# Masked scores computed in quadrants, with k transposed and the states in quarters, in a gated linear attention and SiLU block kernel

## The chip, the cores and the metric

One Trainium2 chip, one of its NeuronCores. The metric is device time in microseconds of the one launch that computes everything, median of several runs. Inside the core, TensorE (PE) multiplies matrices into PSUM, VectorE (DVE) and ScalarE (ACT) do elementwise work and empty PSUM, GpSimd (POOL) sets constants, and SyncE (SP) issues the transfers. Each engine works through its own queue in order; they meet at semaphores.

## The reference

A gated linear attention over 4 batch rows, 8 heads, 768 positions and 48 channels, and then a two-layer block with SiLU over the 3072 tokens. All of it is float32 in the kernel; the weights arrive as float64.

```python
state = np.zeros((B, H, D, D))
for t in range(S):
    state = alpha[:, :, t, :, None] * state + np.einsum('bhd,bhe->bhde', k[:, :, t], v[:, :, t])
    y[:, :, t] = np.einsum('bhd,bhde->bhe', q[:, :, t], state)
x = y.transpose(0, 2, 1, 3).reshape(B * S, H * D)      # 3072 x 384
h = x @ w_in                                           # 384 x 2048
g = h * (1.0 / (1.0 + np.exp(-h)))
out = g @ w_out                                        # 2048 x 384
```

## The kernel before

**Attention, by chunks.** The sequence is cut into six pieces of C = 128 positions; with four batch rows there are NT = 24 chunks, numbered n = 4 ci + b, so that the four batch rows of one piece follow one another. The eight heads are handled as NP = 4 pairs: head 2j of pair j lies in partitions 0 to 47, head 2j + 1 in partitions 64 to 111 (u = 0 and 1). For a chunk, four stages follow one another:

- `products` and `quotient` (from L652): running products of alpha along the 128 positions (a scan on VectorE), and from them kp and qp, k and q scaled so that the product of qp at position t with kp at position s contains the right decay. Both lie channels by positions.
- `scores` (L706): for each pair j and head u a matmul kp by qp gives the 128 x 128 scores, s on the partitions and t on the columns, in two PSUM banks (one for each u, four pairs side by side). L719 copies them out to `g`, multiplied by `mask`, which is 1 where t >= s. For all but the last piece of a batch row, L723 then transposes kp (positions on the partitions) and ScalarE copies it to `kn` (L725). L729 scales the running state `st`.
- `values` (L734): y transposed, channels on the partitions, in groups of 32: v by g, and for ci > 0 `st` by qp on top (L749). ScalarE copies it to `xt` (L754), the input of the second part.
- `states` (L755): kn by v (L764) is added to `st` (L770, VectorE).

`load_v` (L475) brings v of a chunk, positions on the partitions, in one transfer into one of NV = 2 buffers.

**The block of two layers.** The second part is multiplied in groups of four chunks. The first two groups use plain products (`enter_plain`, L807); the later ones use a scheme with fewer products and more sums (`enter`, L830, with VectorE sums at L844, ScalarE copies at L836 and SiLU at L841). The output side is `leave` (L928; L955 for the first half group).

**PSUM.** Eight banks: three for attention (`ps_a`, given out in turn by `ps_attn`), three for the first layer (`ps_m`), two for the output (`ps_o`).

**Order.** A loop over 25 steps runs the stages in four slots; the list `stages` says which stage stands in which slot and for which chunk (lag 1 is the chunk before). After each slot, `fill` issues pieces of the two-layer block until it has kept pace with a due amount. In steps 0 to 3 the order is products, scores, values, states; in steps 4 to 7 scores, products, values, states, each in its own slot; from step 8 on values and states share a slot and the last one holds `quotient`. The queues of the engines follow this program order closely; the framework that builds the program may move an instruction ahead of one that it expects to wait.

Of the kernel before, what the change touches and what calls it, by code (L numbers as in the profile page):

```python
# [8 lines left out]
F32 = mybir.dt.float32  # L9
# [3 lines left out]
AF = mybir.ActivationFunctionType  # L13
ALU = mybir.AluOpType
# [341 lines left out]
def quotients(  # L356
# [22 lines left out]
    C = 128  # L379
# [4 lines left out]
    NKT = HD // 128  # L384
    NFT = DF // 128
    NT = B * NCH
    W = C + 1
    GB = 4
    NG = NT // GB
# [28 lines left out]
    def ps_attn(n=C):  # L418
        return ps_a.tile([128, 512], F32, name="ps_a").rearrange("p (j c) -> p j c", c=n)
# [54 lines left out]

    def load_v(n):  # L475
        c = ctxs.setdefault(n, dict(zip(("ci", "b"), divmod(n, B))))
        rows = slice(c["ci"] * C, c["ci"] * C + C)
        t = c["v"] = vns[n % NV]
        nc.sync.dma_start(t[:, :, 0:D], v[c["b"], :, rows, :].transpose([1, 0, 2]))

    early = []
    wide = moe_w_in.dtype != F32
# [26 lines left out]
    for t in [inv] + seg[1:]:  # L509
        gps.memset(t, 0.0)  # L510


    mask = consts.tile([128, C], F32, name="mask")
# [174 lines left out]
    def quotient(n, sg=None, q=None):  # L688
# [14 lines left out]
            turned(c["q"], q)  # L703
        dve.tensor_tensor(qp, q, qp, ALU.mult)

    def scores(n):  # L706
        c = ctxs[n]
        ci, b = c["ci"], c["b"]
        ps = [ps_attn() for _ in range(2)]


        for j in range(NP):
            for u in range(2):
                r = slice(64 * u, 64 * u + D)
                pe.matmul(ps[u][:, j, :], lhsT=c["kp"][r, j, :], rhs=c["qp"][r, j, :],  # L715
                          start=True, stop=True)
        g = c["g"] = work.tile([128, 2, NP, C], F32, name="g")
        for u in range(2):
            dve.tensor_tensor(g[:, u], ps[u], mask[:, None, :].to_broadcast([128, NP, C]), ALU.mult)  # L719
        if ci < NCH - 1:  # L720
            ps_k = ps_attn()
            for j in range(NP):
                pe.transpose(ps_k[:, j, :], c["kp"][:, j, :], ident)  # L723
            c["kn"] = work.tile([128, NP, C], F32, name="kn")
            act.copy(c["kn"], ps_k)  # L725
        if ci > 0:
            s = st[b].rearrange("p j u e -> p j (u e)")
            for j in range(NP):
                act.mul(s[:, j], s[:, j], c["all"][:, j : j + 1])  # L729
# [4 lines left out]
    def values(n):  # L734

        c = ctxs[n]
        ci, b, g, qp = c["ci"], c["b"], c["g"], c["qp"]
        vn = c["v"].rearrange("p (j u) d -> p j (u d)", u=2)
        s = st[b].rearrange("p j u e -> p j (u e)")
        py = ps_attn()  # L740
        todo = [(3 * j + i, vn[:, j, at : at + 32], g[:, u, j, :])
                for j in range(NP) for i, at, u in ((0, 0, 0), (1, 32, 0), (2, 80, 1))]
        todo += [(3 * j + 1, vn[:, j, 48:80], g[:, 1, j, :]) for j in range(NP)]
        if ci > 0:
            todo += [(3 * j + i, s[:, j, 32 * i : 32 * i + 32], qp[:, j, :])
                     for j in range(NP) for i in range(3)]
        for i, (at, w, x) in enumerate(todo):
            t, at = divmod(at, 4)
            pe.matmul(py[32 * at : 32 * at + 32, t, :], lhsT=w, rhs=x, start=(i < 4),  # L749
                      stop=(i >= len(todo) - 4), skip_group_check=True)  # L750
        half, e = divmod(n, 2)
        if e == 0:
            xts[half] = xtp.tile([128, NKT, TB], F32, name="xt")
        act.copy(xts[half][:, :, e * C : (e + 1) * C], py[:, 0:NKT])  # L754
    def states(n):  # L755
        c = ctxs.pop(n)
        ci, b, vn = c["ci"], c["b"], c["v"]
        if ci < NCH - 1:

            ps = ps_attn()  # L760
            for j in range(NP):
                for u in range(2):
                    r = slice(64 * u, 64 * u + D)
                    pe.matmul(ps[r, j, 0:D], lhsT=c["kn"][:, j, r], rhs=vn[:, 2 * j + u, 0:D],  # L764
                              start=True, stop=True)
# [378 lines left out]
    go_on()  # L1144
    go_on()
    ps = ps_attn()[0:1, 0, 0:1]
    pe.matmul(ps, lhsT=good, rhs=mask[:, C - 1 : C], start=True, stop=True)  # L1147
    dve.tensor_single_scalar(small, ps, 127.5, ALU.is_ge)
    for _ in range(4):
        go_on()  # L1150
# [60 lines left out]
```

## Time and profile before

| | |
|---|---|
| time, median of 3 | 577.69 us (577.37 to 578.81) |
| profiled span | 577.1 us, TensorE clock 1.000 |
| PE busy | 557.6 us, 4450 matmul records |
| VectorE busy | 449.3 us |
| ScalarE busy | 187.6 us |
| scores, L715: 384 records | 30.0 us, mean 292 ns |
| k transposed, L723: 80 records | 13.5 us, mean 293 ns |
| values, L749: 768 + 480 records | 28.8 + 17.0 us, means 282 and 272 ns |
| states, L764: 320 records | 11.9 us, mean 216 ns |
| masking, L719: 48 of 128 x 512 | 31.2 us, mean 685 ns |
| copy of kn, L725: 20 of 128 x 512 | 11.7 us, mean 585 ns |
| v, L479: 24 transfers of 192 KB | 3.5 us from issue to landing, median |

How to read it: PE is TensorE's matmuls, PEld its weight loads, which lie beside them. The means are those of one record from start to end; records overlap, so the time that a stretch takes is read from the starts in the timeline and not from the sum of the means. In the names of a group the output stands left of the arrow and the inputs right of it; `128*48 128x48` is the part of the array that is used (rows*columns) and the shape that streams through. In a table of waits, each line gives the engine and line that waited, whom it waited for, and then the total, the number of times and the longest.

### The profile page before, as it was taken

Reading aid. Unit: us, or ns where it says so; the run is one execution under the profiler, and the core shown is the slowest. Engines: PE = TensorE matmul, PEld = TensorE weight load, DVE = VectorE, ACT = ScalarE, POOL = GpSimd, SP = SyncE. Lnnn points to the kernel's source line nnn. Section 1 sums busy time; section 2 is a strip of 40 time slices with the busy share of each in tenths; the row PEclk is TensorE's granted clock in tenths of the full one; section 3 lists DMA queues with packets and bytes.
Section 4 is the critical chain, followed back from the end, with each engine's and each line's share of the span. In section 5 each row is a group of like instructions: output and inputs, shape, how many; then the busy total and the mean of one; then the engine's idle time right before and its main releaser. Section 6 shows DMA issues by size and latency. Waiting matters only on the chain. (4 is left out here: it accounts for less than half of the span.)

```text
span 577.1 us, 11060 instructions
## 1 busy us (share of the span) xinstructions
PE 557.6 (97%) x4450; PEld 491.2 (85%) x4450; DVE 449.3 (78%) x807; ACT 187.6 (33%) x367; POOL 7.3 (1%) x25
## 2 busy tenths in 40 slices
PE   5999999999999999999999999999999999998976
PEld 4677887678998998898998998998998999997976
DVE  5779798999797699995996995996963856747651
ACT  2345543232221233342442442433342331422100
POOL 5000000000000000000000000000000000000000
PEclk9999999999999999999999999999999999999999
DMA  9998784445445414343324333323210123333321
GB/s 212 169 285 215 212 215 118 102 103 139 103 99 129 116 51 120 107 124 84 103 71 118 101 105 85 101 69 89 65 43 9 52 81 115 93 118 98 98 72 30
DMA packets 93900, 63.72 MB, mean 110 GB/s; under 512 B 54800, under 2 KB 85520, under 8 KB 93840
## 3 DMA queue, kind: packets, MB, share of 16 engines
q1 hardware_dynamic: 93840, 62.94, 42.5%
q8 instruction: 36, 0.59, 0.4%
q14 instruction: 24, 0.20, 0.1%
HBM read 58.20 MB, written 4.72 MB: 109 GB/s over the span
## 5 line engine op out<-in xcount | busy, mean ns | idle before, releaser
L928 PE MATMUL ps_o<-w_out,g 128*128 128x192 f32 x704 | 122.8, 328 | 2.3 <-DVE o L942 2.2
L928 PEld LDWEIGHTS ps_o<-w_out,g 128*128 128x128 f32 x704 | 115.2, 190 | 5.6 <-DVE o L942 3.0
L928 PE MATMUL ps_o<-wt,g 128*128 128x192 f32 x528 | 91.6, 326 | 1.3 <-DVE u L1004 1.3
L807 PE MATMUL ps_m<-xt,w_in 128*128 128x256 f32 x384 | 89.6, 384 | 0.8 <-DVE w_in L604 0.5
L928 PEld LDWEIGHTS ps_o<-wt,g 128*128 128x128 f32 x528 | 87.2, 190 | 3.0 <-DVE u L1004 1.6
L807 PEld LDWEIGHTS ps_m<-xt,w_in 128*128 128x128 f32 x384 | 70.7, 190 | 12.2 <-DVE w_in L604 2.9
L830 PE MATMUL ps_m<-xc,w_in 128*128 128x256 f32 x288 | 70.1, 379 | 0.0
L639 DVE TENSOR_REDUCE seen<-bits 128x1 f32<-128x384 int32 (+2 forms) x65 | 42.4, 689 | 30.4 <-DMA bits<-in_moe_w_out_dram 23.9
L830 PEld LDWEIGHTS ps_m<-xc,w_in 128*128 128x128 f32 x288 | 54.0, 190 | 6.4 <-DVE g L844 0.2
L830 PE MATMUL ps_m<-xc,wx 128*128 128x256 f32 x192 | 50.1, 383 | 0.0
L836 ACT COPY g<-ps_m 128x512 f32<-128x512 f32 x64 | 37.0, 586 | 39.8 <-PE ps_m L830 39.8
L933 DVE TENSOR_TENSOR g<-g 128x512 f32<-128x512 f32 x66 | 44.7, 687 | 4.7 <-PE ps_o L928 4.7
L841 ACT ACTIVATE g<-g 128x1024 f32<-128x1024 f32 x32 | 33.2, 1056 | 44.6 <-DVE g L844 44.6
L729 ACT ACTIVATE st<-st,u 128x96 f32<-128x96 f32 x80 | 26.0, 368 | 53.5 <-DVE u L674 38.8
L844 DVE TENSOR_TENSOR g<-ps_m,g 128x512 f32<-128x512 f32 x56 | 37.6, 684 | 2.9 <-PE ps_m L830 2.7
L830 PEld LDWEIGHTS ps_m<-xc,wx 128*128 128x128 f32 x192 | 35.0, 190 | 4.2 <-issue 0.4
L719 DVE TENSOR_TENSOR g<-ps_a,mask 128x512 f32<-128x512 f32 x48 | 31.2, 685 | 6.4 <-PE ps_a L715 6.1
L674 DVE TENSOR_TENSOR_SCAN u<-al,one 128x516 f32<-128x516 f32 x24 | 29.3, 1224 | 6.2 <-ACT al L671 6.1
L699 DVE TENSOR_TENSOR_SCAN p<-al,inv 128x516 f32<-128x516 f32 x24 | 29.5, 1229 | 4.8 <-PE ps_a L749 4.2
L836 ACT COPY part<-ps_m 128x512 f32<-128x512 f32 x32 | 18.8, 587 | 43.6 <-PE ps_m L830 37.8
L810 ACT ACTIVATE g<-ps_m 128x512 f32<-128x512 f32 x32 | 19.0, 594 | 40.6 <-PE ps_m L807 40.5
L715 PEld LDWEIGHTS ps_a<-p,u 48*128 48x128 f32 x384 | 24.8, 193 | 8.1 <-issue 6.5
(117 smaller groups left out, 635.3 us busy)
## 6 DMA issues: line engine op xcount, KB each, us to landing
bits<-in_moe_w_in_dram SPq DMA_DIRECT2D x24, 512.0 KB, 4.2
bits<-in_moe_w_out_dram SPq DMA_DIRECT2D x32, 384.0 KB, 3.4
at<-in_alpha_dram SPq DMA_DIRECT2D x64, 96.0 KB, 2.3
kt<-in_k_dram SPq DMA_DIRECT2D x64, 96.0 KB, 2.4
qt<-in_q_dram SPq DMA_DIRECT2D x64, 96.0 KB, 2.5
vn<-in_v_dram SPq DMA_DIRECT2D x24, 192.0 KB, 3.5
bits<-in_alpha_dram SPq DMA_DIRECT2D x9, 512.0 KB, 3.9
out_dram<-o SPq DMA_DIRECT2D x48, 96.0 KB, 1.8
```

Source lines behind the costliest of these rows:

```text
L639: dve.tensor_reduce(seen[kind][which][:, i : i + 1], x, axis=AX, op=op, apply_absolute_value=True))
L674: dve.tensor_tensor_scan(u[:, end - 1 :: -1], sg[:, end:0:-1], one[:, end:0:-1], 0.0, ALU.mult, ALU.add)
L699: dve.tensor_tensor_scan(p[:, 0:end], sg[:, 0:end], iv[:, 0:end], 0.0, ALU.mult, ALU.add)
L719: dve.tensor_tensor(g[:, u], ps[u], mask[:, None, :].to_broadcast([128, NP, C]), ALU.mult)
L729: act.mul(s[:, j], s[:, j], c["all"][:, j : j + 1])
L807: pe.matmul(ps[:, e, :], lhsT=w_in[:, t, (f + e) * 128 : (f + e + 1) * 128], rhs=xt[:, t, :], start=(t == 0), stop=(t == NKT - 1))
L830: pe.matmul(ps[:, e], lhsT=block_w(w)[:, 2 * pair + e], rhs=block_x(grp, x), start=(first and e == 0), stop=(e == 1), skip_group_check=True)
L836: act.copy(to, ps)
L841: act.activation(x, x, AF.Silu)
L844: dve.tensor_tensor(to, a, b, op)
L928: pe.matmul(ps, lhsT=x, rhs=w[:, i], start=(first and i == 0), stop=(i == HF - 1), skip_group_check=True)
L933: dve.tensor_tensor(cells(grp, h, pair, *to), cells(grp, h, pair, *x), cells(grp, h, pair, *y), ALU.subtract)
```

## The change

Of the 128 x 128 scores of a head, the part with t < s is masked off; with s and t cut into halves, the block of late s and early t is masked off as a whole. The new form does not compute it. The two halves of s are two matmuls, e = 0 with all 128 columns of t and e = 1 with the last 64. Each uses 48 rows (one head) and 64 columns of the array, a quadrant. So that neither column half of the array gets all the long ones, the halves change places for odd pairs j: the s half e lies in partitions 64 (e ^ j % 2).

What follows from this:
- `mask` gets one version for even and one for odd pairs, and g has its rows swapped for odd pairs. So v must be swapped for odd pairs too, which `load_v` does with six transfers in place of one, and so must the rows of kn.
- The block that is not computed still has to be a finite number before the mask multiplies it by 0. A new stage `blank` takes the two score banks of a chunk ahead of time and has ScalarE write zeros to them. It stands behind `states` or `quotient` of the step before.
- kp is transposed in `values` now, ahead of the values' own matmuls and in the array's shape that these use (128 rows by 32 columns): matmuls with the identity, one for each quarter of the positions.
- The matmuls of `states` are cut to 32 columns as well, so that they have this shape too.

```diff
     def load_v(n):
         c = ctxs.setdefault(n, dict(zip(("ci", "b"), divmod(n, B))))
-        rows = slice(c["ci"] * C, c["ci"] * C + C)
+        x = v[c["b"], :, c["ci"] * C : c["ci"] * C + C, :].rearrange("(g o u) c d -> o g c u d", o=2, u=2)
         t = c["v"] = vns[n % NV]
-        nc.sync.dma_start(t[:, :, 0:D], v[c["b"], :, rows, :].transpose([1, 0, 2]))
+        to = t.rearrange("p (g o u) d -> o g p u d", o=2, u=2)[:, :, :, :, 0:D]
+        for g in range(NP // 2):
+            nc.sync.dma_start(to[0, g], x[0, g])
+            for e in range(2):
+                nc.sync.dma_start(to[1, g, CH * e : CH * e + CH], x[1, g, CH - CH * e : 2 * CH - CH * e])
...
+    mask = consts.tile([128, 2, C], F32, name="mask")
     gps.memset(mask, 1.0)
-    gps.affine_select(mask, mask, pattern=[[1, C]], compare_op=ALU.is_ge, fill=0.0, base=0,
-                      channel_multiplier=-1)
+    for odd in range(2):
+        for e in range(2):
+            m = mask[CH * e : CH * e + CH, odd, :]
+            gps.affine_select(m, m, pattern=[[1, C]], compare_op=ALU.is_ge, fill=0.0,
+                              base=-CH * (e ^ odd), channel_multiplier=-1)
...
+    def blank(n):
+        ps = ctxs[n]["blank"] = [ps_attn() for _ in range(2)]
+        for t in ps:
+            act.activation(t.rearrange("p j c -> p (j c)"), ident[:, 0:1].to_broadcast([128, 4 * C]),
+                           AF.Copy, scale=0.0)
+
     def scores(n):
...
-        ps = [ps_attn() for _ in range(2)]
+        ps = c.pop("blank")
         for j in range(NP):
-            for u in range(2):
-                r = slice(64 * u, 64 * u + D)
-                pe.matmul(ps[u][:, j, :], lhsT=c["kp"][r, j, :], rhs=c["qp"][r, j, :],
-                          start=True, stop=True)
+            for e in range(2):
+                for u in range(2):
+                    r = slice(64 * u, 64 * u + D)
+                    at, s = CH * (e ^ j % 2), CH * e
+                    pe.matmul(ps[u][at : at + CH, j, s:C], lhsT=c["kp"][r, j, s : s + CH],
+                              rhs=c["qp"][r, j, s:C], start=True, stop=True)
...
-        if ci < NCH - 1:
-            ps_k = ps_attn()
-            for j in range(NP):
-                pe.transpose(ps_k[:, j, :], c["kp"][:, j, :], ident)
-            c["kn"] = work.tile([128, NP, C], F32, name="kn")
-            act.copy(c["kn"], ps_k)
...
     def values(n):
...
+        if ci < NCH - 1:
+            ps_k = ps_attn()
+            for j in range(NP):
+                for i in range(4):
+                    at = 32 * (i ^ 2 * (j % 2))
+                    pe.matmul(ps_k[at : at + 32, j, :], lhsT=c["kp"][:, j, 32 * i : 32 * i + 32], rhs=ident,
+                              start=True, stop=True)
+            c["kn"] = work.tile([128, NP, C], F32, name="kn")
+            act.copy(c["kn"], ps_k)
         py = ps_attn()
...
     def states(n):
...
             for j in range(NP):
-                for u in range(2):
-                    r = slice(64 * u, 64 * u + D)
-                    pe.matmul(ps[r, j, 0:D], lhsT=c["kn"][:, j, r], rhs=vn[:, 2 * j + u, 0:D],
+                for i in range(4):
+                    r = slice(32 * i, 32 * i + 32)
+                    pe.matmul(ps[r, j, 0:D], lhsT=c["kn"][:, j, r], rhs=vn[:, 2 * j + i // 2, 0:D],
                               start=True, stop=True)
...
-        stages = [[(scores, 1)], [(products, 0)], [(values, 1)], [(states, 1)]]
+        stages = [[(scores, 1)], [(products, 0)], [(values, 1)], [(states, 1), (blank, 0)]]
         if step < GB:
             stages = stages[1::-1] + stages[2:]
         elif step >= NA:
-            stages = [[(scores, 1)], [(products, 0)], [(values, 1), (states, 1)], [(quotient, 0)]]
+            stages = [[(scores, 1)], [(products, 0)], [(values, 1), (states, 1)], [(quotient, 0), (blank, 0)]]
```

The masking multiply L719 takes the same 512 elements with the pairs viewed as two even and two odd ones.

More of the change, by code (lines that the diff above doesn't have):

```diff
@@ L386, in quotients @@
     NT = B * NCH
+    CH = C // 2
     W = C + 1
@@ L510, in quotients @@
         gps.memset(t, 0.0)
-    mask = consts.tile([128, C], F32, name="mask")
+    mask = consts.tile([128, 2, C], F32, name="mask")
     gps.memset(mask, 1.0)
-    gps.affine_select(mask, mask, pattern=[[1, C]], compare_op=ALU.is_ge, fill=0.0, base=0,
-                      channel_multiplier=-1)
+    for odd in range(2):
[3 more added lines that the diff above has]
+                              base=-CH * (e ^ odd), channel_multiplier=-1)
     st = [fix.tile([128, NP, 2, D], F32, name=f"st{b}") for b in range(B)]
@@ L708, in scores @@
         ci, b = c["ci"], c["b"]
-        ps = [ps_attn() for _ in range(2)]
+        ps = c.pop("blank")
         for j in range(NP):
-            for u in range(2):
-                r = slice(64 * u, 64 * u + D)
-                pe.matmul(ps[u][:, j, :], lhsT=c["kp"][r, j, :], rhs=c["qp"][r, j, :],
-                          start=True, stop=True)
+            for e in range(2):
[4 more added lines that the diff above has]
+                              rhs=c["qp"][r, j, s:C], start=True, stop=True)
         g = c["g"] = work.tile([128, 2, NP, C], F32, name="g")
         for u in range(2):
-            dve.tensor_tensor(g[:, u], ps[u], mask[:, None, :].to_broadcast([128, NP, C]), ALU.mult)
-        if ci < NCH - 1:
-            ps_k = ps_attn()
-            for j in range(NP):
-                pe.transpose(ps_k[:, j, :], c["kp"][:, j, :], ident)
-            c["kn"] = work.tile([128, NP, C], F32, name="kn")
-            act.copy(c["kn"], ps_k)
+            dve.tensor_tensor(g[:, u].rearrange("p (j o) c -> p j o c", o=2),
+                              ps[u].rearrange("p (j o) c -> p j o c", o=2),
+                              mask[:, None, :, :].to_broadcast([128, NP // 2, 2, C]), ALU.mult)
         if ci > 0:
@@ L1146, in quotients @@
     ps = ps_attn()[0:1, 0, 0:1]
-    pe.matmul(ps, lhsT=good, rhs=mask[:, C - 1 : C], start=True, stop=True)
+    pe.matmul(ps, lhsT=good, rhs=mask[:, 0, C - 1 : C], start=True, stop=True)
     dve.tensor_single_scalar(small, ps, 127.5, ALU.is_ge)
```

## The prediction

> **What bounds the kernel now.** I read the busy shares first, then the table of PE's own waits, then stretches of PE's timeline around the stages that the change touches, and last ScalarE's timeline at the same moments. The page's first part:
>
> ```profile
> PE 557.6 (97%) x4450; PEld 491.2 (85%) x4450; DVE 449.3 (78%) x807; ACT 187.6 (33%) x367; POOL 7.3 (1%) x25
> ```
>
> A busy PE can still be a waiting one, so the waits matter more. PE's own, longest first:
>
> ```profile
> PE ps_a L669 <- POOL al L510: 4.1, 1, 4.1
> PE ps_o L928 <- DVE o L942: 2.2, 1, 2.2
> PE ps_a L1147 <- DVE good L1143: 1.6, 1, 1.6
> ```
>
> All of these lie in the first 40 us or after 530 us. In between, the table by stretches (columns: stretch, its length, then busy time with the number of instructions for PE, PEld, DVE, ACT, POOL, then clock, DMA share, GB/s) has PE full:
>
> ```profile
> 300.00:400.00 100.00, 100.00 (x868) 91.31 (x867) 84.79 (x145) 36.47 (x72) 0.00 (x0) 1.00 0.38 101
> ```
>
> So from 60 us to 530 us the time is PE's instruction stream laid end to end at full clock: a nanosecond added to or taken from it is a nanosecond of the result. What must be priced is PE's stretches around scores (L715), k transposed (L723), values (L749) and states (L764). PE's timeline (start, length, line, output<-inputs, array tile, shape, count):
>
> ```profile
> 305.77 0.81 PE L928 MATMUL ps_o<-wt,g 128*128 128x192 f32 x4
> 306.51 1.08 PE L749 MATMUL ps_a<-g,vn 128*32 128x128 f32 x32
> 307.41 0.84 PE L749 MATMUL ps_a<-p,st 128*32 128x128 f32 x24
> 308.18 0.56 PE L764 MATMUL ps_a<-vn,kn 128*48 128x48 f32 x16
> 308.67 0.70 PE L830 MATMUL ps_m<-xc,wx 128*128 128x256 f32 x2
> ...
> 315.69 1.03 PE L830 MATMUL ps_m<-xc,w_in 128*128 128x256 f32 x4
> 316.65 1.16 PE L715 MATMUL ps_a<-p,u 48*128 48x128 f32 x16
> 317.74 0.66 PE L723 MATMUL ps_a<-ident,u 128*128 128x128 f32 x4
> 318.23 0.98 PE L928 MATMUL ps_o<-w_out,g 128*128 128x192 f32 x5
> ...
> 401.91 1.03 PE L830 MATMUL ps_m<-xc,w_in 128*128 128x256 f32 x4
> 402.87 1.16 PE L715 MATMUL ps_a<-p,u 48*128 48x128 f32 x16
> 403.96 2.22 PE L928 MATMUL ps_o<-w_out,g 128*128 128x192 f32 x12
> ```
>
> How to read it. A f32 matmul leaves two records (two passes): a chunk has 8 score matmuls and 16 records. A transpose leaves one: 4 and 4. A record starts 0.16 us after the one before it for 192 columns ((0.81-0.33)/3) and 0.21 us for 256, so a pass streams a column in 0.83 ns and 128 columns in 0.107 us. The scores' 16 passes go two at a time (two row halves): 16/2 x 0.112 = 0.90 us. The values' passes go four at a time (four groups of 32 columns): 0.109 us for each four. The states' passes (48 columns, 0.040 us) go two at a time: 0.045 us a pair. What is left over between stretches of different array tile is switching.
>
> From these lines, section by section, measured from the end of the stream before to the effective start of the stream after:
> - Section A, scores and k transposed: L830's last pass starts at 316.34 and streams to 316.55; L928 starts at 318.23. A = 1.68 us. Without the transposes (last chunk of each batch row, 402.77 to 403.96 plus 0.10 for L928's first weights) it is 1.29 us, of which 0.90 is scores and 0.39 switching in and out.
> - Section B, values and states: L928's last pass ends at 306.41, L830 is effective at 308.78. B = 2.36 us: 56/4 x 0.109 = 1.53 values, 8 x 0.045 = 0.36 states, about 0.15 switching between the two (128x32 to 128x48 tiles), 0.32 switching in and out.
>
> **What the Trainium skill says.**
> - "TensorEngine Tiling (Array Packing)", Key Properties: changing the tiling mode drains TensorE, and tiles work independently. The trace agrees: 0.15 to 0.2 us for each change of tile shape, and four values passes side by side. That 64x64 quadrants do so too is stated there and seen in no run here.
> - The same page, Restrictions under Tile-to-Partition Mapping: column tiling disables the transpose mode for f32 input. So the k of the new form cannot be the one-pass transpose of L723; it is a common f32 matmul, two passes.
> - "TensorE: Matmul & The Clock Gate", section "Wait — 56ns, not 53.3ns?": starts of matmuls never come closer than about 25 ns. The trace differs a little: the states' 16 passes come at (0.56-0.21)/15 = 23 ns. Whether 32 may come at 11 ns no run shows yet.
> - "ScalarE: Activation LUTs", What ACT_TABLE_LOAD costs: an activation with immediate scale takes 186 ns + 0.833 ns per element, 0.61 us for 512. The copy L725 of that size takes 0.59 us here.
>
> **The change part by part.**
> (1) Scores in quadrants. Each chunk has 32 passes, half of 128 columns and half of 64, with the swap giving every quadrant 4 + 4: 4 x 0.112 + 4 x 0.058 = 0.68 us instead of 0.90. The bounds are 0.64 (no step cost) and 0.90 (long and short passes do not overlap). The first weight load has 64 columns and not 128, 0.05 us less. Section A becomes 0.39 - 0.05 + 0.68 = 1.02 to 1.03 us: -0.65 us in the 20 chunks that had transposes, -0.26 us in the last 4.
> (2) k transposed beside the values. 4 pairs x 4 quarters x 2 passes = 32 passes, four at a time: 8 x 0.109 = 0.87 us, where the transposes cost 4 x 0.109 = 0.44.
> (3) States in quarters. 32 passes for 16, but four at a time: still 8 x 0.045 = 0.36 us, if passes may be issued at 11 ns. Since the tile shape is that of the values, the 0.15 us switch between them goes. Section B becomes 2.36 - 0.15 + 0.87 = 3.08 us, +0.72 us in 20 chunks.
> PE's sum: 20 x (-0.65 + 0.72) - 4 x 0.26 = 1.4 - 1.0 = +0.4 us. The scores' gain is spent on the second pass of k.
> (4) A new wait. Before, kn was copied (L725) in the scores' step, and states came some 10 us later. Now PE makes k at the start of section B, ScalarE copies it, and the states need it behind the values. In the trace the copy L725 starts 0.31 us after the last transpose does (318.12 to 318.43) and takes 0.59. In new section B, counted from its first record, the last k pass starts at 0.81, so kn is there at about 1.8 us and the values end at 2.43: 0.6 us to spare, if ScalarE is free by 1.8. ScalarE is in order, and the activations of L841 queue there, waiting for VectorE:
>
> ```profile
> 240.26 1.06 ACT L841 ACTIVATE g<-g 128x1024 f32<-128x1024 f32 x1 [4.03 <-DVE g L844]
> 241.78 2.00 ACT L841 ACTIVATE g<-g 128x1024 f32<-128x1024 f32 x2 [0.47 <-DVE g L844]
> 243.69 0.46 ACT L754 COPY xt<-ps_a 128x384 f32<-128x384 f32 x1
> ```
>
> That section B starts at 240.74, so the activations end 3.05 us into it; kn would come at 3.7 and PE would stand 1.25 us, with the queue of w_out products behind the waiting states. At 284, 328 and 371 us they end 1.97 us in: kn at 2.6, a stall of 0.2 each. In the other eight steady chunks ScalarE is free. Together +1.8 us.
> In the chunks before 130 us the same can happen on a larger scale:
>
> ```profile
> 109.95 0.64 ACT L729 ACTIVATE st<-st,u 128x96 f32<-128x96 f32 x2 [5.04 <-DVE u L681]
> 110.50 0.46 ACT L754 COPY xt<-ps_a 128x384 f32<-128x384 f32 x1
> ```
>
> Section B started there at 105.69, and ScalarE was held 4 to 5 us by a wait for VectorE; at 120 us the same, by output buffers. Each would cost up to 2.8 us. There the values and the states stand in different slots, with filler pieces allowed between, so some of it is filled. Bounds 0 and 5.6; I take 0.8.
> (5) Blanks: 48 x 0.59 = 28 us more of ScalarE, from 33% to 37% busy. Each pair comes behind L754, and the next ScalarE work in the steady stretch comes 2.4 to 3.3 us after that copy, so 1.2 us fits in the gap and costs nothing. The two score banks that they hold were free for that time anyway (three banks, and the products of these steps use none). In the first 60 us ScalarE also converts weights, which PE waited for (2.9 us in all); I allow 0.2.
> (6) v in six transfers for one: 120 more issues of 0.38 us on SyncE, which waits most of the time; v is needed two steps after its load. Only in the first 20 us, where SyncE issues without pause, can the ten more issues (3.8 us at most) push back the loads of the third chunk; the rings are backed up there anyway (each issue takes 0.8 to 3 us). Bounds 0 and 3; I take 0.3.
> (7) The mask multiply keeps its 512 elements (0.685 us), and the larger mask is made at the start on GpSimd (0.3 us an operation), behind loads. Nothing.
> Sum: +0.4 + 1.8 + 0.8 + 0.2 + 0.3 = +3.5 us, 577.7 to 581.2 us.
>
> **The rivals.**
> - R1, no measurable change: the compiler's order puts kn's copy ahead of the late activations, or filler behind the values, and only PE's sum remains: 577.7 + 0.4 + 0.5 = 578.6. For it: ScalarE is free in most chunks. Against: the trace shows it held at xt in ten of 24.
> - R2, issue-bound: passes cannot come closer than 25 ns. States take 32 x 0.025 = 0.80 us, +0.44 x 20 = 8.8; scores 0.80, +0.12 x 24 = 2.9. That gives 581.2 + 11.7 = 592.9. For it: the skill's floor. Against: 23 ns is already seen, and a group of values passes starts within 21 ns.
> - R3, faster: k in quarters costs as little as the transposes (one pass, or two overlapped in the same time), -0.44 x 20 = -8.7 us: 572.5. For it: the same output size on the same array. Against: every column-tiled matmul in the trace has two passes of 0.109 us.
>
> **How the numbers follow.** Forecast 0.50, R1 0.22, R2 0.13, R3 0.15. 576.0 to 579.4 us counts as same. Faster: R3, and a sliver of R1 with scores at 0.64 us: 0.17. Same: the rest of R1 and a little of the forecast's lower end: 0.23. Slower: 0.60. The range leaves out R3's lower half and R2's upper half: 572.5 to 588.5.
>
> **What would show it.** Right: in the changed trace PE's stretch at L715 shortens from 1.16 to about 0.9 us with 32 passes; a k stretch of 32 passes lasts 0.87 us before the values; states follow without a switch, 32 passes in about 0.55; the section between is 3.1 us where kn is in time, and longer, with a PE wait on kn's copy, where L841 runs late. Wrong: states or scores passes at 25 ns (R2), k passes at half the time (R3), or no wait on kn at all (R1); blanks that PE waits for would be a cost that I have put at nothing.

## The result, and the profile after

The changed kernel takes 585.62 us (584.53 to 586.44, four runs) where the kernel before took 577.65 us: ratio 1.0133, 95% interval 1.011 to 1.0156. It is slower by 7.9 us, more than twice the 3.5 us forecast, though on the forecast's side and inside its range.

The page's first part for the changed kernel, and its row for the stretch from 300 to 400 us (columns as before):

```profile
PE 558.7 (96%) x5714; PEld 496.8 (85%) x5714; DVE 453.8 (78%) x807; ACT 212.0 (36%) x415; POOL 8.3 (1%) x28
```

```profile
300.00:400.00 100.00, 100.00 (x1088) 92.01 (x1087) 87.94 (x150) 39.86 (x77) 0.00 (x0) 1.00 0.37 97
```

PE's busy time has grown by 1.1 us, the span by 7.6 us. So most of the loss is not work but standing still, and it isn't to be found where PE is full. PE's own waits, longest first, some left out, show where:

```profile
PE ps_a L678 <- DMA an<-in_alpha_dram: 4.4, 2, 4.2
PE ps_a L774 <- DVE g L738: 3.5, 3, 2.6
...
PE ps_a L734 <- ACT st L797: 1.3, 1, 1.3
...
PE ps_a L734 <- DVE p L713: 1.2, 1, 1.2
PE ps_a L789 <- ACT kn L764: 0.9, 1, 0.9
PE ps_m L855 <- DVE g L869: 0.9, 2, 0.5
PE ps_a L789 <- ACT ps_a L719: 0.8, 1, 0.8
```

Lines have moved: scores are L734 now, the mask multiply L738, k transposed L761, kn's copy L764, values L774, states L789, blanks L719. The first 4.4 us are the wait for the first input, which the kernel before had too (there released by GpSimd, 4.1). Grown or new are the waits of values and scores for VectorE and ScalarE, all in the first 60 us (before, values waited 0.7 and 0.3 us and scores not at all), and the two of the states (L789), at 97 and 250 us.

When does the loss arise? The table gives the start of the last record of a chunk's scores in PE's timeline, and then the difference from the kernel before; the last column is PE's last end:

| chunk n | 1 | 3 | 4 | 5 | 6 | 8 | 13 | 14 | 20 | 23 | end |
|---|---|---|---|---|---|---|---|---|---|---|---|
| before, us | 22.3 | 47.0 | 66.8 | 82.7 | 98.4 | 128.5 | 229.6 | 251.8 | 382.4 | 445.5 | 571.7 |
| changed, difference | -1.4 | -4.1 | +3.7 | +4.0 | +5.2 | +5.2 | +5.6 | +7.5 | +8.2 | +7.4 | +7.5 |

+5.2 us stand by chunk 8, and +2.2 us come after it. (Up to chunk 4 the kernel's order is looser, and a single difference there says little.)

**The steady part.** PE's timeline of the changed kernel, a section B and a section A:

```profile
291.47 1.08 PE L761 MATMUL ps_a<-ident,u 128*32 128x128 f32 x32
292.36 1.06 PE L774 MATMUL ps_a<-g,vn 128*32 128x128 f32 x32
293.24 0.84 PE L774 MATMUL ps_a<-p,st 128*32 128x128 f32 x24
293.96 0.55 PE L789 MATMUL ps_a<-vn,kn 128*32 128x48 f32 x32
294.44 2.87 PE L953 MATMUL ps_o<-w_out,g 128*128 128x192 f32 x16
...
302.43 0.90 PE L734 MATMUL ps_a<-p,u 48*64 48x128 f32 x32
303.26 1.13 PE L855 MATMUL ps_m<-xc,wx 128*128 128x256 f32 x4
```

k takes 292.36 - 291.47 = 0.89 us for 32 passes. Section B, from its first start to the start of what follows, is 294.44 - 291.47 = 2.97 us, where before it was 308.67 - 306.51 = 2.16: +0.81, of which 0.06 is a wait for kn (the states start 0.72 us behind the second group of values, and 0.66 where kn is long there, as the experiment with the states in quarters alone shows). Section A was 318.23 - 316.65 = 1.58 us and is 0.83, with 0.10 of the next stream's weights to add (1.13 for a four where 1.03 is usual): -0.65, of which 0.25 are the quadrants, as an experiment below shows, and the rest the transposes that have moved to section B. The 32 passes of the states come at (0.55 - 0.21)/31 = 11 ns.

**The wait for kn.** PE's timeline and then ScalarE's around the stall that was forecast at 240 us:

```profile
244.08 1.13 PE L855 MATMUL ps_m<-xc,w_in 128*128 128x256 f32 x4 [0.46 <-DVE g L869]
...
246.68 1.08 PE L761 MATMUL ps_a<-ident,u 128*32 128x128 f32 x32
...
250.19 0.55 PE L789 MATMUL ps_a<-vn,kn 128*32 128x48 f32 x32 [0.90 <-ACT kn L764]
```

```profile
247.66 2.00 ACT L866 ACTIVATE g<-g 128x1024 f32<-128x1024 f32 x2 [0.40 <-DVE g L869]
249.57 0.57 ACT L764 COPY kn<-ps_a 128x512 f32<-128x512 f32 x1
```

PE is done with k at 247.8 us, the late activations (now L866) hold ScalarE until 249.57, kn is there at 250.14, and the states start at 250.19. That is the mechanism of step (4), in the place that it named. A second wait of L855 came with it: the changed kernel has two here, of 0.46 and 0.41 us, and the kernel before one of 0.41. Together they make most of the jump of 1.9 us between chunks 13 and 14.

**The start.** SyncE's transfers from 8 us on in the changed kernel, and then in the kernel before (start, time in which SyncE was issuing, count):

```profile
8.12 0.43 SPq L482 DMA_DIRECT2D vn<-in_v_dram  x1
8.59 1.45 SPq L484 DMA_DIRECT2D vn<-in_v_dram  x2
...
16.05 1.25 SPq L484 DMA_DIRECT2D vn<-in_v_dram  x2
17.43 0.52 SPq L457 DMA_DIRECT2D an<-in_alpha_dram  x1
```

```profile
7.86 2.40 SPq L479 DMA_DIRECT2D vn<-in_v_dram  x2
10.38 3.07 SPq L456 DMA_DIRECT2D an<-in_alpha_dram  x1
```

The v of two chunks took SyncE 2.5 us and takes 9.3, and alpha of the third chunk is asked for 7.05 us later. An issue into half the partitions (L484) takes 602 ns at the median, one into all 128 took 391, though it carries 24 KB and not 192. The stretch from 14 to 20 us in the changed kernel, in the kernel before, and in the changed kernel with v in one transfer (the first experiment below):

```profile
14.00:20.00 6.00, 3.47 (x74) 2.94 (x78) 5.16 (x9) 1.96 (x5) 0.00 (x0) 0.54 0.38 66
```

```profile
14.00:20.00 6.00, 5.33 (x60) 3.73 (x59) 4.22 (x8) 1.57 (x4) 0.00 (x0) 1.00 1.50 163
```

```profile
14.00:20.00 6.00, 3.49 (x67) 2.96 (x68) 5.13 (x9) 2.01 (x5) 0.00 (x0) 0.62 1.47 166
```

While SyncE hands out the small pieces, the DMA engines move 66 GB/s instead of 163. But PE's lower busy time here, and its lower clock, don't come from that: with one transfer the engines move 166 GB/s, and PE is busy as little, at a mean clock of 0.62. Nor is time lost here. L774 waits 2.6 us for g at 16.5 us in both forms, the longest of its waits, and still the last 28 records of the first chunk's values start at 17.69 us in the changed kernel and at 17.66 in the other two.

Nor does the late alpha make the third chunk late. VectorE's last step for its p, in the changed kernel and before:

```profile
26.38 0.69 DVE L713 TENSOR_TENSOR p<-ps_o,p 128x512 f32<-128x512 f32 x1
```

```profile
26.01 0.69 DVE L704 TENSOR_TENSOR p<-ps_o,p 128x512 f32<-128x512 f32 x1
```

That is 0.37 us later for an alpha that was asked for 7.05 us later; with one transfer this step starts at 27.64, later still. Of the three, PE waits for it in the changed kernel alone, because there eight records of the third chunk's scores stand ahead of 24 records of the first layer. In the changed kernel, and then before:

```profile
27.22 0.55 PE L734 MATMUL ps_a<-p,u 48*64 48x128 f32 x8 [1.17 <-DVE p L713]
27.70 5.45 PE L832 MATMUL ps_m<-xt,w_in 128*128 128x256 f32 x24
```

```profile
26.87 5.49 PE L807 MATMUL ps_m<-xt,w_in 128*128 128x256 f32 x24
...
32.84 0.71 PE L715 MATMUL ps_a<-p,u 48*128 48x128 f32 x6
```

So the start is not the old order with later loads: PE's records come in another order, and v's transfers alone are enough for that, as the counts further below show. (The framework may move instructions, as said of the kernel before.) That bears on every experiment with v below.

### The profile page after: what moved, and what is told of

The parts are those of the page before. It is cut to its first block, busy times and chain, and to the rows that moved or that the text cites. A ratio compares the mean times of both kernels' runs of the same rounds, so it can differ in the third digit from the quotient of the medians.

```text
span 584.7 us, 13874 instructions
## 1 busy us (share of the span) xinstructions
PE 558.7 (96%) x5714; PEld 496.8 (85%) x5714; DVE 453.8 (78%) x807; ACT 212.0 (36%) x415; POOL 8.3 (1%) x28
## 5 line engine op out<-in xcount | busy, mean ns | idle before, releaser
L953 PE MATMUL ps_o<-w_out,g 128*128 128x192 f32 x704 | 124.7, 331 | 2.9 <-DVE o L967 2.9
L832 PEld LDWEIGHTS ps_m<-xt,w_in 128*128 128x128 f32 x384 | 71.2, 190 | 11.3 <-DVE w_in L613 1.2
L855 PE MATMUL ps_m<-xc,w_in 128*128 128x256 f32 x288 | 70.1, 379 | 0.5 <-DVE g L869 0.5
L855 PEld LDWEIGHTS ps_m<-xc,w_in 128*128 128x128 f32 x288 | 54.0, 190 | 7.0 <-DVE g L869 0.8
L866 ACT ACTIVATE g<-g 128x1024 f32<-128x1024 f32 x32 | 33.2, 1056 | 59.8 <-DVE g L869 59.8
L855 PE MATMUL ps_m<-xc,wx 128*128 128x256 f32 x192 | 50.5, 386 | 0.0
L744 ACT ACTIVATE st<-st,u 128x96 f32<-128x96 f32 x80 | 27.3, 370 | 31.7 <-DVE u L683 26.2
L855 PEld LDWEIGHTS ps_m<-xc,wx 128*128 128x128 f32 x192 | 34.9, 190 | 4.5 <-issue 0.4
L738 DVE TENSOR_TENSOR g<-ps_a,mask 128x512 f32<-128x512 f32 x48 | 31.1, 685 | 2.8 <-PE ps_a L734 2.5
L774 PE MATMUL ps_a<-g,vn 128*32 128x128 f32 x768 | 28.3, 280 | 3.5 <-DVE g L738 3.5
```

The lines of the kernel that those rows point to most:

```text
L738: dve.tensor_tensor(g[:, u].rearrange("p (j o) c -> p j o c", o=2), ps[u].rearrange("p (j o) c -> p j o c", o=2), mask[:, None, :, :].to_b ...
L832: pe.matmul(ps[:, e, :], lhsT=w_in[:, t, (f + e) * 128 : (f + e + 1) * 128], rhs=xt[:, t, :], start=(t == 0), stop=(t == NKT - 1))
L855: pe.matmul(ps[:, e], lhsT=block_w(w)[:, 2 * pair + e], rhs=block_x(grp, x), start=(first and e == 0), stop=(e == 1), skip_group_check=True)
L866: act.activation(x, x, AF.Silu)
L953: pe.matmul(ps, lhsT=x, rhs=w[:, i], start=(first and i == 0), stop=(i == HF - 1), skip_group_check=True)
```

## The experiments

Ratios are to the kernel before on the same chip, with their 95% interval. "Chunk 8" is the difference of the table above at n = 8.

**v in one transfer again.** The changed kernel with the transfer of before. v's rows aren't swapped for odd pairs then, so those heads multiply rows that don't belong together; the amount of work is the same.

```diff
...
-        for g in range(NP // 2):
-            nc.sync.dma_start(to[0, g], x[0, g])
-            for e in range(2):
-                nc.sync.dma_start(to[1, g, CH * e : CH * e + CH], x[1, g, CH - CH * e : 2 * CH - CH * e])
+        nc.sync.dma_start(t[:, :, 0:D], v[c["b"], :, rows, :].transpose([1, 0, 2]))
```

> The changed kernel with v brought in by one transfer for each chunk, as before. The rows of v are then not swapped for odd pairs, so that half of the heads multiply the wrong rows; the amount of work is the same. In the changed kernel the third chunk's alpha is asked for at 17.4 us, before at 10.4, because twelve transfers of v stand ahead of it on SyncE, and by 66 us the changed kernel is 4.4 us behind. Theory V (the six transfers cause the loss at the start): about 4 us come back, 581 to 582 us, and scores of the fifth chunk start near 66 us. Theory B (the blanks on ScalarE) or K (kn late where PE has no other work): nothing comes back, 585 to 586 us.

Measured: 1.0070 (1.0052 to 1.0089), chunk 8 at +2.6 us. The six transfers, with all that follows from them, are worth 1.0133 - 1.0070 = 0.63%, 3.6 us (1.9 to 5.4 by the two intervals; 2.6 us at chunk 8 and 2.7 at chunk 23 in the traces), nearly half of the loss.

**Six transfers alone.** The kernel before, with v brought by the same six transfers, unswapped.

> The kernel before, with v brought in by six transfers for each chunk, in unswapped order. Theory V: 581 to 582 us, 4 us slower than before, all of it lost by 70 us. Theories B and K: 577.5 to 578.2 us.

Measured: 1.0201 (1.0168 to 1.0235). Chunk 1 is at +4.2, chunk 4 at +12.1, chunk 8 at +12.5, and chunk 23 still at +12.5. So the 120 added issues cost nothing whatever from chunk 8 on; all of it arises at the start. Theory V named the place, but its 4 us are a third of the 11.5 measured. PE's busy time is 565.7 us here and was 557.6 for the same 4450 records, so a PE that counts as busy is not always one that gets on. The clock falls in this kernel too, but from 40 to 50 us (0.54 on average), and from 14 to 20 us it stays at 1.00.

**Blanks alone.** The kernel before, with the stage `blank` and its place in the order, and nothing else.

> The kernel before, with the two score banks of each chunk taken a step earlier and written with zeros by ScalarE (48 activations more, 28 us of ScalarE), and all else as before. Theory B: 580 to 582 us, lost in the first 70 us. Theories V and K: 577.7 to 578.3 us, since ScalarE is at a third of its time and each pair stands in a gap.

Measured: 1.0012 (0.9998 to 1.0026), chunk 8 at +0.1, chunk 23 at +0.2. The blanks are hidden.

**k transposed in the scores' step again.** The changed kernel with the one-pass transposes back where they were; the swap of kn's rows for odd pairs is made by ScalarE, in three copies of which two move 64 partitions to the other 64.

```diff
+            for j in range(NP):
+                pe.transpose(ps_k[:, j, :], c["kp"][:, j, :], ident)
...
+            act.copy(to[:, 0], x[:, 0])
+            for h in range(2):
+                act.copy(to[CH * h : CH * h + CH, 1], x[CH - CH * h : 2 * CH - CH * h, 1])
```

> The changed kernel with k transposed in the scores' step again, by one-pass transposes; the swap of the halves for odd pairs is made in ScalarE's copy to kn, which becomes three copies of half the size. Scores stay in quadrants, states in quarters next to the values. By the sections, 0.87 us go from section B and 0.39 to 0.44 come back in section A: -0.45 x 20 = -9 us, and the waits for kn (1.1 us at 250, 1.0 at 97, some 0.4 elsewhere) go: 573 to 574 us under theory V or B, which leave the loss at the start. Theory K: the start comes back as well, 569 to 570 us. If the second pass of k were not the price, 583 us or more.

Measured: 1.0007 (0.9994 to 1.0019), a gain of 1.26% or 7.3 us on the changed kernel where 11.6 to 12.6 were expected. Chunk 8 is at +5.8, chunk 23 at +1.4. From chunk 8 on it gains 4.4 us on the kernel before where the changed kernel lost 2.2, and the jump at chunk 14 is 0.5 instead of 1.9. The loss by chunk 8 stays as large, so kn's late copy doesn't make it; one wait of 2.0 us for the mask multiply, at 104.6 us, is part of it here.

**The same with v in one transfer** (v's rows are wrong for odd pairs, as above).

> k transposed in the scores' step, and v by one unswapped transfer (the swapped pairs multiply the wrong rows of v; the amount of work is the same). Only the quadrant scores, the states in quarters and the blanks are left of the change. By the sections: 24 x -0.26 for scores and 20 x -0.15 for the switch, -9.2 us, to 0.984 of before if the start costs nothing; theory V with the loss of about 3 us at the start that the one-transfer form of the changed kernel still shows: 0.989 to 0.991. If the start loses as much as with six transfers: 1.000.

Measured: 0.9904 (0.9887 to 0.992), chunk 8 at +0.1. Against the first experiment, which differs in k alone, this is 1.66% or 9.6 us, for the second pass of k (R3 put it at 8.7) and the wait for kn; by the traces 6.7 of it arise between chunks 8 and 23, 2.5 before and 2.2 after. Against the experiment before this one, which differs in v alone, six transfers cost 1.03% here. Section A of this version shows what the quadrants bring by themselves, since the transposes stand in it again:

```profile
292.60 0.90 PE L730 MATMUL ps_a<-p,u 48*64 48x128 f32 x32
293.43 0.66 PE L740 MATMUL ps_a<-ident,u 128*128 128x128 f32 x4
293.93 1.03 PE L850 MATMUL ps_m<-xc,wx 128*128 128x256 f32 x4
```

It is 293.93 - 292.60 = 1.33 us, where before it was 1.58: 0.25 us per chunk for the quadrants. They are one part of the 0.9904; the states in quarters are the other, and are tried alone below.

**v in three transfers.** If the halves change places for pairs 2 and 3 instead of 1 and 3, and the pairs are multiplied in the order 0, 2, 1, 3, then v needs three transfers. First in the changed kernel, then with k transposed in the scores' step.

```diff
-        for j in range(NP):
+        for j in (0, 2, 1, 3):
...
-                    at, s = CH * (e ^ j % 2), CH * e
+                    at, s = CH * (e ^ j // 2), CH * e
...
+        nc.sync.dma_start(t[:, 0:NP, 0:D], x[:, 0:NP])
+        for e in range(2):
+            nc.sync.dma_start(t[CH * e : CH * e + CH, NP:H, 0:D], x[CH - CH * e : 2 * CH - CH * e, NP:H])
```

> The changed kernel with the swap in the last two pairs and v by three transfers. Theory V: half of the 0.63% that one transfer brought back, so about 1.010 of before. Rival (the loss depends on the order into which the start falls, and not on the number of transfers): anything from 1.006 to 1.014, unrelated to the number.

> The kernel with k transposed in the scores' step again, and the halves swapped for the last two pairs in place of the odd ones, so that v comes by three transfers a chunk. Theory V (the loss at the start grows with the number of v transfers on SyncE): between the six-transfer form (0.07% over before) and the one-transfer form, 0.3 to 0.4% under before. If only the place of the swap or the size of the transfers mattered, no difference from the six-transfer form.

Measured: 1.0084 (1.0065 to 1.0103), chunk 8 at +2.9; and 0.9965 (0.9953 to 0.9977), chunk 8 at +2.4, chunk 23 at -2.1. The second, with quadrant scores and v swapped, beats the kernel before.

**States in quarters alone.** The kernel before with only the matmuls of `states` cut to 32 columns.

```diff
-                for u in range(2):
-                    r = slice(64 * u, 64 * u + D)
-                    pe.matmul(ps[r, j, 0:D], lhsT=c["kn"][:, j, r], rhs=vn[:, 2 * j + u, 0:D],
+                for i in range(4):
+                    r = slice(32 * i, 32 * i + 32)
+                    pe.matmul(ps[r, j, 0:D], lhsT=c["kn"][:, j, r], rhs=vn[:, 2 * j + i // 2, 0:D],
```

> The kernel before with only the states' matmuls cut to quarters. My sections price the switch between values and states at 0.15 us: where states follow values directly (17 chunks) it goes, and 32 passes take the time of 16: -2.6 us, 0.9955 of before. If passes could not come closer than 25 ns, 0.44 us more for each of 20 chunks: 1.010.

Measured: 0.9945 (0.9928 to 0.9962), 575.66 us where the kernel before took 579.08 on that chip. PE's timeline of it:

```profile
305.20 1.08 PE L749 MATMUL ps_a<-g,vn 128*32 128x128 f32 x32
306.10 0.84 PE L749 MATMUL ps_a<-p,st 128*32 128x128 f32 x24
306.76 0.52 PE L764 MATMUL ps_a<-vn,kn 128*32 128x48 f32 x32
307.21 1.13 PE L830 MATMUL ps_m<-xc,wx 128*128 128x256 f32 x4
```

307.21 - 305.20 = 2.01 us where it was 2.16: twice the passes in less time, because the switch to another tile shape is gone. 0.55% of 579 us is 3.2, where 17 x 0.15 = 2.6 was expected. In the trace 1.9 us of the gain stand by chunk 23; the other 1.4 arise behind it, where PE's waits for VectorE (L928) are 2.2 us in all instead of 3.5. No version with quadrant scores that swaps v properly did better than this one edit. Against the 0.9904 of the version above with v in one transfer, some 0.4%, 2.4 us, are left for the quadrants, less than 24 x 0.25 = 6.0; from chunk 8 to chunk 23 the two traces differ by 3.2 us, 0.21 per chunk.

**v on another queue.** The version in three transfers with k transposed in the scores' step, and v asked for by GpSimd; by ScalarE for the first two chunks; by ScalarE for the first eight.

> As the form with k transposed in the scores' step and v by three transfers, but v's transfers are issued by GpSimd, which has nothing else to do. Theory V in the form that SyncE's issue time is what delays the loads behind: as with one transfer, 0.989 to 0.992 of before. If it is the transfers themselves that take the DMA engines' time: as with three on SyncE.

> As the form with k transposed in the scores' step and v by three transfers (0.9965 of before), but the six transfers of the first two chunks' v are issued by ScalarE, which is idle then. Theory V in the form that SyncE's issue time at the start is the loss: two thirds of what lies between three transfers and one come back, 0.991 to 0.994 of before, and the third chunk's alpha is asked for near 8 us and not at 12.6. If the loss comes from v's later transfers: 0.9965.

> As the one before, with v of the first eight chunks on ScalarE's queue. Theory V: as with one transfer, 0.990 to 0.992. Rival: each issue waits on ScalarE for the buffer of v and holds back copies that PE waits for: 0.997 or more.

Measured: 1.0026 (1.0012 to 1.004), 0.9974 (0.9965 to 0.9984) and 0.9996 (0.9985 to 1.0008), against 0.9965 with SyncE: no gain. The first fits neither of its theories. With GpSimd PE waits 5.0 us for k at the start. With ScalarE v is asked for at 0.8 us, beside inputs that are needed first, and PE's first transpose starts at 5.36 us instead of 4.09.

**g swapped instead of v.** The kernel before with quadrant scores, blanks and states in quarters; the mask multiply puts the halves of odd pairs back in their place (three operations of VectorE for one), so that v and kn stay as they were.

> Quadrant scores with the halves put back in natural order by the masking multiply: for odd pairs VectorE writes each half to the other half's partitions. v comes by one transfer and k by plain transposes in the scores' step. No loss at the start, but six multiplies of half size for two, 1.15 us more of VectorE for each chunk, 27.6 us in all, 78% to 83% busy. If VectorE stays off the path: 0.990 of before. If PE waits for it: over 0.997.

Measured: 1.0222 (1.0205 to 1.0239). PE is busy for 556.8 us, 0.8 less than before, and VectorE for 482.2, 33 us more. PE waits for it (for g, 2.8 us in L783, 2.7 in L849 and 2.7 in L674), and chunk 9 is at +18.5, chunk 23 at +15.9: this loss too lies in the first chunks. The clock stood at a half for 24 us of the first 120 in this trace; what that adds was not separated.

**The second chunk's v asked for later,** behind alpha, k and q of the third chunk, so that these are no longer held back: in the changed kernel, in the version of three transfers, and in the kernel before with six.

```diff
-    for n in range(NV):
-        load_v(n)
+    load_v(0)
...
+                    if n == 0:
+                        load_v(1)
```

> The changed kernel (six transfers of v a chunk), with the second chunk's v asked for after the third chunk's alpha, k and q and not before. If the place of v ahead of the third chunk's loads on SyncE's queue is the loss: half or more of the 0.63% comes back, 1.007 to 1.010 of before. If the sheer number of issues in the first 40 us is the loss, wherever they stand: 1.012 to 1.014.

> The form with k transposed in the scores' step and v by three transfers (0.9965 of before), with the second chunk's v behind the third chunk's loads. By place: 0.992 to 0.995. By number: 0.9965.

> The kernel before with six unswapped transfers of v (1.020 of before), with the second chunk's v behind the third chunk's loads. By place: the larger part of the 2% comes back, 1.003 to 1.010. By number: 1.018 to 1.022.

Measured: 1.0134 (1.0096 to 1.0172) and 0.9973 (0.996 to 0.9985), the same as without; but 1.0047 (1.0031 to 1.0063) in place of 1.0201. Asking for it later takes away most of the cost in the kernel before, and none of it in the changed one. The first of the three also clears the clock: over the first 70 us it was granted 1.00 (1.00 before, 0.95 in the changed kernel), and the loss is the same. The reverse is on record too: the version of 0.9904 had its clock at a half from 14.3 to 21.1 us and stood at +0.1 at chunk 8.

**The weights taken out of SyncE's queue.** In these kernels the loss at chunk 8 goes, roughly, with the time at which SyncE asks for the first piece of w_out:

| kernel | first w_out, us | chunk 8, us |
|---|---|---|
| before | 46.6 | 0 |
| k in the scores' step, v in one | 47.8 | +0.1 |
| changed, v in one | 48.0 | +2.6 |
| changed | 59.5 | +5.2 |
| changed, second v later | 59.7 | +5.6 |
| before, v in six, second v later (profiled run 0.6% above its median) | 60.2 | +3.6 |
| before, v in six | 66.6 | +12.5 |

Others don't fit: v by ScalarE for eight chunks stands at 49.1 and +6.0, v by GpSimd at 48.9 and +4.2, and g swapped at 54.4 and +14.9. And that a late weight causes the loss doesn't follow, since a late PE also frees the weights' buffers late. So the fetches were given to GpSimd, in the kernel before, in the same with six transfers, and in the changed kernel.

> The kernel before with the fetches of the weights issued by GpSimd instead of SyncE, so that they no longer stand behind the attention's loads. It is the yardstick for the next two. SyncE's queue holds back no weight that PE needs in the kernel before (PE's waits on weights are 2 us in all), so both theories expect about the same time as before: 0.995 to 1.004, and the first fetch of w_out no later than 46.6 us.

> The same with v in six unswapped transfers. Theory W (the six transfers cost because they hold back the weights that stand behind them in SyncE's order): against the previous run the 2% shrinks to under 0.5%: ratio to before at most 1.005 if the previous run is at 1.000, and chunk 8 is reached at most 3 us later than there. Rival S (the loss arises at the start, from the attention's own loads and the clock that falls while PE waits): still 1.015 to 1.02, chunk 8 reached over 9 us later.

> The changed kernel with the fetches of the weights issued by GpSimd. Theory W: the share of the six transfers goes, so about 1.007 where the unaltered changed kernel has 1.0133 (the ratio that one transfer for v gave), chunk 8 at +2.6 us or less where it was at +5.2. Rival S: unchanged, 1.011 to 1.015, chunk 8 at +5.

Measured: 1.0169 (1.0134 to 1.0203), 1.0197 (1.0162 to 1.0233) and 1.033 (1.0279 to 1.0381); chunk 8 at +7.9, +10.2 and +18.5. The yardstick failed: GpSimd asks for the first weights at 2.0 us, and PE then waits for q of the first chunk (landing at 11.3 us where it was 6.4) and for k of the third (waits of the kernel before with this edit):

```profile
PE ps_o L669 <- DMA kn<-in_k_dram: 7.0, 2, 6.5
PE ps_o L669 <- DMA qn<-in_q_dram: 4.5, 1, 4.5
```

Between the first two, six transfers cost 0.28%, less than the intervals can tell from nothing, and 2.3 us at chunk 8, as theory W has it. But the changed kernel stands 10.6 us behind the first of the three there, which neither theory has. So W isn't shown.

## Why the prediction was right or wrong

- **Steps (1) to (3), PE's work: right.** The stretches came out as listed under what would show it: 0.90 us for scores, 0.89 for k, 0.55 for states without a switch. Section A -0.65 us as forecast, of it -0.25 by the quadrants, for -0.26. Section B +0.75 without its wait, against +0.72. The sum, 20 x 0.10 - 4 x 0.26, is +1.0 us for a forecast +0.4; between chunks 8 and 13 the trace shows 0.08 per chunk. R2 falls: the passes come at 11 ns. The section "Wait — 56ns, not 53.3ns?" of "TensorE: Matmul & The Clock Gate" in the Trainium skill, on which R2 stood, speaks of 25 ns; here, with four tiles side by side, the measurement decides. R3 falls: k has two passes, and the experiment with the transposes back shows what they cost.
- **Step (4), the wait for kn: right in place and cause.** At 250 us 1.2 us in the row of the weight loads (0.9 in that of the matmuls) where 1.25 was forecast, with 0.46 more on L855 that was not; at each of the three later places 0.06 to 0.07 for 0.2. R1 falls with it. Of the early waits, estimated at 0.8 within 0 to 5.6, one shows, 0.8 at 97 us, and that the number agrees is luck: kn's copy ends at 96.35, the blank behind it at 96.98, and the states start at 97.08, with the blank named as the releaser.
- **Steps (5) and (7): right in the total.** The blanks alone make no measurable change (1.0012, the interval holding 1); in the changed kernel PE waits for one of them, as just said, which the prediction had put at nothing. No wait on the mask shows. The larger mask has one effect that was not forecast: GpSimd's work at the start ends at 9.20 us instead of 7.91, and a step of VectorE that took 0.17 us takes 1.09 beside it. By 17.7 us PE is level again.
- **Step (6), v in six transfers, priced at +0.3 us: this is the step that failed.** Measured: 0.63%, 3.6 us (1.9 to 5.4), twelve times the price and about its upper bound of 3. The forecast named the right loads. But it took 0.38 us per issue from the transfer into 128 partitions, where the new ones take 0.49 and 0.60, so that ten more issues came out at 3.8 us at most; the delay was 7.05. And it argued that the rings were backed up anyway, so that SyncE's time didn't matter. With small pieces they were not: the DMA engines ran at 66 GB/s instead of 163. Yet the delay is not what PE pays: the third chunk's p is 0.37 us later, not 7. What the step has no term for is that other loads make the framework lay out the start anew. With 3.6 in place of 0.3 the sum is +6.8 us, and 7.9 was measured.

What is shown: the edit of v's transfers costs, and it costs at the start only. By which way is not settled. The same 120 issues cost 2.0% in the kernel before, 0.47% there with the second v later, 0.28% with the weights on GpSimd, 0.63% in the changed kernel and 1.03% in it with k back in the scores' step. Neither the place of the second v nor the clock nor the weights' place in SyncE's queue explains all five.

One rival stands untested: the order itself, since the framework gives the start another one when its loads change. Compared by name and shape, one by one, 437 of PE's 5714 records stand elsewhere in the one-transfer form of the changed kernel, and 223 of 4450 in the kernel before with six transfers, all of them in the first 100 us. Where the order stays, the cost is small: between the two kernels before with the weights on GpSimd no record of PE stands elsewhere, and six transfers cost 0.28%; and asking for the second v later in the version of three transfers moves 39 of 5154 records and changes nothing (0.9965 and 0.9973). No run held the order fixed in the changed kernel.

The 2.6 us that the changed kernel loses by chunk 8 with v in one transfer are likewise not traced to one wait, and were not forecast in full: steps (1) to (5) put some 1.5 us there (8 x 0.07, 0.8 and 0.2).

## What to carry to other kernels

Don't price new transfers at the start of a kernel by their bytes or their landing: here an issue took 0.49 to 0.60 us where 0.39 was usual, and other loads gave the start another order, whose price no sum of waits foretold. Look at whether the order has changed before a difference is put down to a delay. A saving that needs its operands rearranged is worth what is left after the rearrangement: the quadrants brought 0.25 us per chunk, the second pass of k took about 0.5 (0.89 in section B against 0.40 for the transposes), and the swapped v took its share on top. Try the side effects of a change alone; here the states in quarters, which were only meant to fit beside k, are the part that pays without a price (0.9945).

## What the runs showed of the hardware that was not expected

- Four quadrants of 48 x 64 run side by side: passes of 128 and of 64 columns, balanced by the swap, put 16 + 16 passes between 302.43 and 303.26 us, with the switches in and out; in the kernel before the 16 of 48 x 128 stood from 402.87 to 403.96.
- A transfer of 24 KB into 64 partitions holds SyncE for 602 ns at the median, one of 48 KB into 128 partitions for 486, and one of 192 KB into 128 partitions for 391: fewer bytes took longer. Which part of the form makes it was not tried. GpSimd takes 621 ns (64 partitions) and 756 (128) in the version of three transfers.
- The clock granted to PE fell to a half at the start of most of these kernels, for 3.4, 6.8 or 10.2 us at a time: from 14.5 to 21.3 us in the changed kernel, from 40.9 to 51.1 in the one before with six transfers, not at all before 570 us in the kernel before. It doesn't go with the loss: with the same 6.8 us at a half, chunk 8 stood at +0.1 (v in one transfer, k in the scores' step) and at +5.2 (changed), and with none at +5.6 (second v later). What makes it fall was not tried.
- A step of VectorE went long beside GpSimd's writes. In nine runs with the larger mask, VectorE's first step on `least` (128 x 4) started at 7.9 to 8.1 us, while GpSimd was still writing zeros, and took 1.07 to 1.34 us; it ended within 0.03 us of GpSimd's last write (9.18 to 9.23). In five runs with the old mask GpSimd was done by 7.92, and in two with the larger one VectorE's step began only after 9.8; all seven steps took 0.17 us. Other steps of VectorE ran beside GpSimd's writes without that, so it is not a rule for every pair.
- In the versions with k back in the scores' step, ScalarE's copy from one half of the partitions to the other took 367 ns for 64 x 256, no more than the 369 ns of the copy of 128 x 256 that stays in place, and after 100 us no wait of PE for kn is left.
